# A one-core decode kernel of four layers: 30 K/V slots filled by halves, and an order planned with clocks of queues and fetches

## Chip, core and metric

One core of one Trainium2 chip. The metric is the device time of one execution in microseconds; three runs of the kernel before gave 314.23 (median), 312.15 and 315.84.

## What is computed

Eight independent rows `x` of 448 numbers (bf16) pass through attention, an MLP, the same attention and the same MLP. Weights and caches are shared by both rounds.

```python
W = min(4096, max(256, Sk // 4))                  # 1024 of 4096 positions
q = (x @ wq)                                      # 16 heads of 256
k, v = the last W rows of the caches              # 8 K/V heads, each for two q heads
p = _softmax(q k^T * Dh ** -0.5); o = p v
A(x) = o @ wo;   B(x) = _silu(x @ w1) @ w2        # F = 1792
x = x + A(_layernorm(x)); x = x + B(_layernorm(x))
x = x + A(_layernorm(x)); x = x + B(_layernorm(x))
```

K and V of one row are 16 blocks of 1024 x 256 numbers, 0.5 MB each: 67 MB in all, beside 10.55 MB of weights. Both attention rounds of a row use the same blocks, so each is loaded once.

## The kernel before

**Staging.** The weights stay in SBUF. K and V blocks go through 27 slots (`R`, L271). The loads are issued by SP in a fixed sequence (`pump`, L818): wq, the 8 K blocks of row 0, wo, its 8 V blocks, w1 and w2, then K and V of row 1 and so on. Load n takes the slot of load n-27 and waits for that slot's last reader. `load_k` (L432) writes runs of 4 KB, `load_v` (L438 and L444) runs of 1 KB, each with one transfer a slot. A V slot holds 256 positions of four heads (heads 0 to 3) or one whole head (4 to 7).

**One row, or batch.** `layer1` (L831) transposes the K slots in place on VectorE (L839, 16 halves), makes scores (`scores`, L570; eight matmuls of 256 columns, four at a time in quarters of the array), softmax (L580: row maximum, two small 32x32 transposes, exp, four transposes of the probabilities, sums), then p v. Heads 0 to 3 go by rows (`pv_rows`, L627), heads 4 to 7 by columns (`pv_cols`, L656: V is the weight operand, 16 matmuls a head, then an eviction L662 and that head's share of wo, L699). `chain` (L719) goes on from wo's four partial rows: `fold` (L711) evicts them (L713) and adds them into columns of 112 numbers, mean and variance come from small matmuls (L670, L678), 1/sqrt from Ln and Exp on ScalarE (L684, L686), w1 from 56 matmuls of 32 columns (`proj`, L468), silu from exp, a copy and a reciprocal (L733 to L738), w2 by rows (L741), `fold` again, then q of the second round: wq (L755) in two halves, each evicted (L760), turned (L763), copied (L766), spread (L549) and masked (L553). Layer-2 scores free the K slots, `pv_rows` of layer 2 the V slots. After row 7 the last wo, MLP and the output are made for all 8 rows together (`final_wo` L770, `final_rows` L779).

**Order.** Every operation is a task with an engine, a duration, reads and writes. `Plan.schedule` (L78) ranks the tasks by the longest path behind them, with fixed latencies between engines, and places each in the earliest gap of its engine; `emit` (L167) writes every engine's list with semaphore waits. Each engine runs its list in order. While PE would be idle in the chain, `keep` (L704) puts in matmuls that add zero.

Of the kernel before, what the change touches and what calls it, by code (L numbers as in the profile page):

```python
# [6 lines left out]
BF16 = mybir.dt.bfloat16  # L7
F32 = mybir.dt.float32
U32 = mybir.dt.uint32
ALU = mybir.AluOpType  # L10
# [3 lines left out]
SEM_LAT = {"pe": 0.05, "dve": 0.04, "act": 0.04, "pool": 0.06, "sp": 0.06}  # L14
LAT = {"pe": 0.15, "dve": 0.07, "act": 0.09, "pool": 0.05, "sp": 0.0}
LOAD_MARGIN = 1.5


class Task:
    __slots__ = ("eng", "fns", "dur", "prio", "name", "deps", "idx", "ready", "end", "sem", "val",  # L20
                 "vc", "n_bytes", "start", "users", "rank")
# [9 lines left out]
class Plan:  # L31
# [3 lines left out]
    def __init__(self, nc):  # L35
        self.nc = nc
        self.tasks = []
        self.last_w = {}
        self.readers = {}
        self.dma_sems = {}  # L40

    def add(self, eng, fns, reads=(), writes=(), dur=0.1, prio=0.0, name="", n_bytes=0, dma_key=None):
# [5 lines left out]
        t.idx = len(self.tasks)  # L48
        t.sem = dma_key
# [13 lines left out]
        for k in writes:  # L63
            if k in self.last_w:
                dep(self.last_w[k], True)
            for r in self.readers.get(k, ()):
                dep(r, False)
# [10 lines left out]
    def schedule(self, dma_lat=2.1):  # L78


        tasks = self.tasks
# [5 lines left out]
        sp_next = [t for t in tasks if t.eng == "sp"]  # L87
        nxt = {}
        for a, b in zip(sp_next, sp_next[1:]):
            nxt[a.idx] = b  # L90
        for t in reversed(sorted(tasks, key=lambda t: t.idx)):
# [4 lines left out]
            if t.eng == "sp":  # L96
                own = t.dur
                t.rank = max(own + dma_lat + r, (own + nxt[t.idx].rank) if t.idx in nxt else 0.0)
            else:
                t.rank = t.dur + r  # L100
        gaps = {e: [[0.0, 1e9]] for e in ("pe", "dve", "act", "pool")}
        sp_pos, sp_free, dma_free = 0, 0.0, 0.0
        heap, seq = [], 0

        def push(t):
            heapq.heappush(heap, ((-t.rank if t.eng != "sp" else -1e9), t.idx, t))

        def ready_of(t):
            r = 0.0
            for o, raw in t.deps.values():  # L110
                if o.eng != t.eng or o.eng == "sp":
                    lat = LOAD_MARGIN if o.eng == "sp" and t.eng == "dve" else LAT[o.eng]
                    r = max(r, o.end + lat + SEM_LAT[t.eng])
                elif raw and t.eng in ("dve", "act"):
# [4 lines left out]

        for t in tasks:  # L120
            if n_left[t.idx] == 0 and t.eng != "sp":
                push(t)
        if n_left[sp_next[0].idx] == 0:
            push(sp_next[0])
        done = 0
        while heap:
            _, _, t = heapq.heappop(heap)
            r = ready_of(t)
            if t.eng == "sp":
                t.start = max(r, sp_free)  # L130
                sp_free = t.start + 0.6
                s = max(t.start + 0.3, dma_free)
                dma_free = s + t.dur
                t.end = dma_free + dma_lat
                sp_pos += 1
                if sp_pos < len(sp_next) and n_left[sp_next[sp_pos].idx] == 0:
                    push(sp_next[sp_pos])
            else:
                g = gaps[t.eng]
                for k, (g0, g1) in enumerate(g):  # L140
                    s = max(g0, r)
                    if s + t.dur <= g1 + 1e-9:
                        break
                t.start, t.end = s, s + t.dur
                new = []
                if s - g0 > 0.02:
                    new.append([g0, s])
                if g1 - t.end > 0.02:
                    new.append([t.end, g1])
                g[k:k + 1] = new  # L150
            done += 1
            for u in succ[t.idx]:
                n_left[u.idx] -= 1
                if n_left[u.idx] == 0:
                    if u.eng != "sp":
                        push(u)
# [748 lines left out]
```

## Time and profile before

| | |
|---|---|
| median of three runs | 314.23 us |
| profiled execution, first to last instruction (span) | 307.8 us |
| profiled execution, its own time | not listed apart from the span |
| PE / VectorE / ScalarE / GpSimd busy | 218.9 / 147.1 / 69.3 / 10.5 us |
| moved by SP's queue | 77.68 MB, packets' time 73.3% of the span |
| granted PE clock, mean | 0.839 |

Engines are PE (matmul; PEld its weight loads), DVE (VectorE), ACT (ScalarE), POOL (GpSimd), SP. A row of a group reads: line, engine, operation, output<-inputs, shapes, count | busy us, mean ns of one | idle time of the engine just before and what ended it. A window row reads: from:to, length, busy time and count of the five engines (PE, PEld, DVE, ACT, POOL), granted clock, share of the 16 DMA engines, GB/s. A wait row reads: total us, times, longest. An arrow names what ended a wait.

### The profile page before, as it was taken

The numbers are of one execution on the slowest core, as the hardware profiler recorded it, in microseconds if no ns is written. First come the engines' busy times: TensorE is split into PE (matmuls) and PEld (weight loads), VectorE is DVE, ScalarE is ACT, GpSimd is POOL, SyncE is SP. The second block draws the span as 40 slices with busy tenths as digits, with TensorE's granted clock in tenths as the row PEclk, the third lists the DMA queues.
The fourth block names the chain that finished last, engine by engine and source line by source line (L and its number), as shares of the span: only waits on it lengthen the run. The fifth ranks groups of instructions, "written<-read, shape, count | busy, mean of one in ns | idle before, by whom it ended". The sixth has DMA issues, their size and how long they took to land.

```text
span 307.8 us, 9763 instructions
## 1 busy us (share of the span) xinstructions
PE 218.9 (71%) x4402; PEld 126.5 (41%) x4402; DVE 147.1 (48%) x436; ACT 69.3 (23%) x203; POOL 10.5 (3%) x22
## 2 busy tenths in 40 slices
PE   1052357675798778868796968788878897888683
PEld 1051113433454456345434634554455345443363
DVE  6049400158317934882487269427744674111113
ACT  2000100121312240423132223312231224022111
POOL 0002000000000000010001000000000000000000
PEclk9999999998675999799579999985799579657555
DMA  7999999999995199949955994999099919000000
GB/s 202 292 399 385 372 348 266 333 405 352 372 402 192 21 355 404 317 138 372 402 192 169 377 398 155 308 399 371 21 317 403 365 35 321 5 2 2 0 5 1
DMA packets 49977, 78.30 MB, mean 254 GB/s; under 512 B 2176, under 2 KB 40848, under 8 KB 49488
## 3 DMA queue, kind: packets, MB, share of 16 engines
q1 hardware_dynamic: 49936, 77.68, 73.3%
q8 instruction: 34, 0.56, 0.8%
q14 instruction: 7, 0.06, 0.0%
HBM read 77.67 MB, written 0.01 MB: 252 GB/s over the span
## 4 chain that ended last, share of the span: by engine, by line
PE 53%; DVE 14%; SPq 13%; ACT 10%; DMA 5%; issue 5%; ACTq 0%
PE bank L627 9%; SPq L444 8%; PE bank L468 7%; PE bank L570 6%; PE bank L699 5%; DVE slot L839 5%; PE bank L755 5%; DMA w_sb<-in_B_w_dram 5%; PE bank L656 4%; PE bank L706 4%; PE bank L741 4%; SPq L432 2%; ACT e_sb L590 2%; DVE qbd L553 2%; PE bank L595 2%
## 5 line engine op out<-in xcount | busy, mean ns | idle before, releaser
L839 DVE STREAM_TRANSPOSE slot<-slot 128x512 uint32<-128x512 uint32 x128 | 81.9, 686 | 9.4 <-DMA slot<-in_A_k_cache_dram 9.2
L570 PE MATMUL bank<-slot,qbd 128*8 128x256 bf16 x1024 | 41.0, 300 | 19.6 <-DVE mseg L576 8.9
L570 PEld LDWEIGHTS bank<-slot,qbd 128*8 128x8 bf16 x1024 | 24.7, 90 | 30.9 <-DVE mseg L576 10.1
L627 PE MATMUL bank<-slot,pT_sb 128*2 128x256 bf16 x768 | 30.6, 304 | 6.8 <-DMA slot<-in_A_v_cache_dram 3.9
L706 PE MATMUL bank<-sel,cols_b 128*128 128x480 bf16 x64 | 27.3, 524 | 2.6 <-DVE vneg L729 2.6
L590 ACT ACTIVATE e_sb<-bank,mb 128x256 bf16<-128x256 f32 x32 | 13.4, 471 | 42.9 <-DVE mb L586 42.8
L627 PEld LDWEIGHTS bank<-slot,pT_sb 128*2 128x2 bf16 x768 | 16.6, 88 | 14.8 <-DMA slot<-in_A_v_cache_dram 5.5
L713 ACT ACTIVATE rowb<-bank 128x448 bf16<-128x448 f32 x16 | 8.7, 544 | 61.9 <-PE bank L699 44.8
L699 PE MATMUL bank<-wo_sb,oT 128*1 128x448 bf16 x256 | 21.4, 435 | 1.6 <-issue 0.9
L656 PE MATMUL bank<-pT_sb,slot 128*128 128x2 bf16 x512 | 17.6, 164 | 4.2 <-issue 2.9
L656 PEld LDWEIGHTS bank<-pT_sb,slot 128*128 128x128 bf16 x512 | 15.3, 98 | 12.3 <-issue 9.9
L755 PE MATMUL bank<-wq_sb,xn 112*1 112x512 bf16 x256 | 20.3, 448 | 0.1
L608 DVE TENSOR_REDUCE l_sb<-bank 128x16 f32<-128x64 f32 x16 | 3.6, 225 | 35.0 <-PE bank L603 26.6
L468 PE MATMUL bank<-xbt,w_sb 112*128 112x32 bf16 (+1 forms) x504 | 16.7, 182 | 3.2 <-ACT xbt L722 1.9
L576 DVE TENSOR_REDUCE mseg<-bank 128x1 f32<-128x256 f32 x32 | 13.1, 413 | 11.3 <-PE bank L570 11.3
L662 DVE TENSOR_TENSOR oT<-bank,rl_sb 128x4 bf16<-128x4 f32 x32 | 5.2, 163 | 25.6 <-PE bank L656 25.6
L538 POOL TENSOR_TENSOR qbd<-q1s,mask 128x256 bf16<-128x256 bf16 x16 | 9.8, 613 | 215.4 <-PE bank L570 192.9
L640 DVE TENSOR_TENSOR oT<-bank,rl_sb 128x16 bf16<-128x16 f32 x24 | 5.0, 208 | 25.4 <-PE bank L636 24.8
L468 PEld LDWEIGHTS bank<-xbt,w_sb 112*128 112x128 bf16 x504 | 15.1, 102 | 4.0 <-ACT xbt L722 2.4
L760 ACT ACTIVATE rowb<-bank,rstd 128x512 bf16<-128x512 f32 x16 | 11.0, 687 | 20.1 <-PE bank L755 20.1
L634 ACT ACTIVATE o_sb<-bank 128x256 bf16<-128x256 f32 x24 | 9.2, 384 | 27.5 <-PE bank L627 27.2
L595 PE MATMUL bank<-ident,e_sb 128*128 128x128 bf16 x64 | 7.2, 243 | 11.1 <-ACT e_sb L590 11.1
(117 smaller groups left out, 195.5 us busy)
## 6 DMA issues: line engine op xcount, KB each, us to landing
slot<-in_A_k_cache_dram SPq DMA_DIRECT2D x64, 512.0 KB, 11.0
slot<-in_A_v_cache_dram SPq DMA_DIRECT2D x64, 512.0 KB, 8.6
wq_sb<-in_A_wq_dram SPq DMA_DIRECT2D x4, 896.0 KB, 9.7
wo_sb<-in_A_wo_dram SPq DMA_DIRECT2D x1, 3584.0 KB, 26.9
w_sb<-in_B_w_dram SPq DMA_DIRECT2D x2, 1568.0 KB, 16.4
qbd<-in_A_x_dram SPq DMA_DIRECT2D x1, 7.0 KB
out_dram<-e_sb SPq DMA_DIRECT2D x1, 7.0 KB
```

The costliest lines, as they stand in the source:

```text
L444: dma(lambda e: e.dma_start(slots[s][:, :].rearrange("v (j n) -> v j n", j=4), src.rearrange("j (v uh) d -> v j (uh d)", uh=2)), [("slot", ...
L468: fns.append(lambda e, o=o, i=i: e.matmul(bank[bank_i][:, col + (o - outs[0]) * n:col + (o - outs[0] + 1) * n], lhs(o, i), rhs(i).broadcas ...
L570: fns.append(lambda e, cb=cb, par=par, j=j, kvh=kvh, kv=kv: e.matmul(bank[sc][32 * j:32 * j + 8, k2 * 256:(k2 + 1) * 256], qbd[qi][:, kvh, ...
L576: dve(lambda e: e.tensor_reduce(mseg[layer][:, k2:k2 + 1], bank[sc][:, k2 * 256:(k2 + 1) * 256], AX.X, ALU.max, negate=True), bk(sc), [("m ...
L590: act(lambda e, k2=k2: e.activation(e_sb[ei][:, k2, :, :].rearrange("p uh (jj ul) -> p uh jj ul", ul=4), bank[sc][:, k2 * 256:(k2 + 1) * 2 ...
L595: pe([lambda e, c=c: e.matmul(bank[lb][:].bitcast(BF16)[:, c * P:(c + 1) * P], e_sb[ei][:, c // 2, c % 2, :], ident[:, :], is_transpose=Tr ...
L627: fns.append(lambda e, q=q, uh=uh, j=j, vv=vv: e.matmul(bank[ob][32 * j:32 * j + 2, c0:c0 + DH], pT_sb[ei][:, k2 * 2 + uh, j * 8 + 2 * q:j ...
L656: fns.append(lambda e, a=a, q=q, uh=uh: e.matmul(bank[vb][:, c0 + 2 * a:c0 + 2 * a + 2], vs[:, (2 * q + uh) * DH + a * P:(2 * q + uh) * DH ...
L699: fns.append(lambda e, i=i, c=c, kvh=kvh: e.matmul(bank[XB][32 * c:32 * c + 1, 0:D], oT1[:, i % 2, i // 2:i // 2 + 1], wo_sb[:, i * D:(i + ...
L706: pe([lambda e: e.matmul(bank[YB][:, 32:512], zero_b.broadcast_to([P, P]), sel[:].rearrange("p c m -> p (c m)")[:, 0:480], start=False, st ...
L755: pe([lambda e, j=j, c=c, k2=k2, wb=wb: e.matmul(bank[wb][32 * j:32 * j + 1, :], xn[0:CP, c:c + 1], wq_sb[0:CP, c, (4 * k2 + j) * 512:(4 * ...
L839: dve(lambda e, v=v: e.transpose(v, v), [("slot", s)], [("slot", s)], 0.67, prio, "KT")
```

## The change

- **Slots and loads.** 30 slots in one ring tensor. Each slot is filled by two transfers of 256 KB, with runs of 2 KB for both K and V. A half's load also waits until the half ten places ahead of it has landed (`ahead`), so at most ten are under way. V blocks are all whole heads. wo is loaded after the first V. wq and w1 lie on 128 partitions (448 = 3 x 128 + 64, the last part folded in two), wo in pairs of rows, w2 in one run a partition.
- **Norms.** Column sums of the weights carry the mean (q and w1 are made from x as it is, and mean times column sum is added behind). The variance comes from one set of matmuls; 1/sqrt from an integer guess and two Newton steps, on VectorE for the MLP, on GpSimd for attention, where it is applied as the scale of exp and not to q.
- **MLP.** w1 by rows: x is the weight operand, 16 matmuls of 448 columns, four at a time, and one 32x32 block transpose brings the result into columns. silu is tanh and one product.
- **Attention.** Scores of the first round: both halves in matmuls of 512 columns. p v by rows in matmuls of 512 columns (two positions at a time, added later); only head 7 of the first round goes by columns. q of the second round is turned by a block transpose of the PSUM bank. In row 7 the second round's softmax goes in two halves.
- **Shared homes.** Scratch tiles lie in K/V slots that are not in use at the start or the end, or in each other's place.
- **Order.** The planner follows a clock of 3.413 us windows for PE, a clock for each of 16 queues, and a cost for every 128 PE instructions fetched. It runs forward once, ranks the tasks by a backward run (`tails`) with written offsets by name and batch, runs again, and then applies a written list of moves. `fill` matmuls, which add zero, go where the plan has PE idle and the streamed columns of the last 3.4 us below a target; `keep` is left in the last row only.

```diff
+SEM_LAT = {"pe": 0.05, "dve": 0.05, "act": 0.05, "pool": 0.08, "sp": 0.1}
+LAT = {"pe": 0.17, "dve": 0.07, "act": 0.09, "pool": 0.08, "sp": 0.0}
+SWITCH = 0.1
+FETCH = (128, 1.4, 0.26)
+WINDOW, WARM, ACTIVE, PACED = 3.413, 43.0, 3072.0, 50.0
+FIRST, LANDED = 1.2, 1.5
+HOLDS = (("PVc0", 1, "oTc0", 1), ("s12", 1, "hT", 1), ("wq", 2, "qbd", 1))
+HELD = ("KT", "max0")
...
+    def tails(self, stay=0.3):
...
+    def best_schedule(self, filler):
+
+        self.schedule(filler, look=LOOKS[0])
+        tails = self.tails()
+        self.schedule(filler, {t.idx: tails[t.idx] + OFFSETS[max(0, t.batch - 5)].get(t.name.split(".")[0], 0.0)
+                               for t in self.tasks if t.idx in tails}, look=LOOKS[1])
+        for e, moves in MOVES.items():
+            by_idx = {t.idx: t for t in self.order[e]}
+            for pair in moves.split():
+                i, before = (int(x) for x in pair.split(":"))
+                self.order[e].remove(by_idx[i])
+                self.order[e].insert(self.order[e].index(by_idx[before]) if before >= 0 else len(by_idx), by_idx[i])
...
+                    queue = [max(t.start + FIRST, x) + t.dur for x in queue]
+                    t.end = max(queue) + LANDED
+                    release(t)
...
+                while n_fetch >= FETCH[0]:
+                    n_fetch -= FETCH[0]
+                    queue[n_block % 16] = max(queue[n_block % 16], best.start + FETCH[2]) + FETCH[1]
+                    n_block += 1
...
+    R = 30
+    PAD = 24
+    AHEAD, WHOLE = 10, 0
+    NJ, PAIR0, PAIR1, NR2, WQS = 3, 1, 0, 14, 0
...
+        if ahead:
+            n = n_bytes // (W * DH)
+            if len(started) > ahead - n:
+                t.deps[started[n - 1 - ahead].idx] = (started[n - 1 - ahead], True)
+            started.extend([t] * (n - 1))
...
     def load_k(s, b, kvh):
-        dma(lambda e: e.dma_start(slots[s][:, :].rearrange("p (u d) -> p u d", d=DH),
-                                  A_k_cache[b, kvh, S0:SK, :].rearrange("(p u) d -> p u d", p=P)),
-            [("slot", s)], W * DH * 2, "slot%d" % s)
-
+        for h in range(2):
+            dma(lambda e, h=h: e.dma_start(slots[s][:, 1024 * h:1024 * h + 1024], src[:, 1024 * h:1024 * h + 1024]),
+                [("slot", s, h)], W * DH, "slot%d_%d" % (s, h), rate=400e3, ahead=AHEAD)
...
+    def load_v(s, b, kvh):
+        src = A_v_cache[b, kvh, S0:SK, :].rearrange("(h p u) d -> h p (u d)", h=2, p=P)
+        for h in range(2):
+            dma(lambda e, h=h: e.dma_start(slots[s][:, 1024 * h:1024 * h + 1024], src[h]),
+                [("slot", s, h)], W * DH, "slot%d_%d" % (s, h), rate=400e3, ahead=AHEAD)
...
+    def rsqrt(eng, nv, y, t, nk, key, hold):
+
+        eng(lambda e: e.tensor_scalar(y.bitcast(I32), nv.bitcast(I32), -0.5, GUESS, op0=ALU.mult, op1=ALU.add),
...
+        one = len(nv.shape) == 2 and nv.shape[1] == 1
+        for i, c in enumerate(NEWTON):
+            if one and eng is dve:
+                eng(lambda e: e.scalar_tensor_tensor(out=t, in0=y, scalar=y, in1=nv, op0=ALU.mult, op1=ALU.mult),
+                    [(key, "y"), nk] + hold, [(key, "t")], 0.22, "nt")
...
+                eng(lambda e, c=c: e.scalar_tensor_tensor(out=y, in0=t, scalar=c, in1=y, op0=ALU.add, op1=ALU.mult),
+                    [(key, "t"), (key, "y")] + hold, [(key, "y")] + ([key] if i else []), 0.16, "ns")
...
+    def w1_rows(bi, lhs, n, key_of, name):
+
+        for i, c0, c1 in ((0, 0, 4), (1, 0, 4), (2, 0, 4), (3, 0, 2), (3, 2, 4)):
+            k = part(i, c0 > 0)
+            pe([lambda e, i=i, k=k, c=c: e.matmul(
+                bank[bi][32 * c:32 * c + n, 0:FN], lhs(k),
+                w1_sb[:, i * F + c * FN:i * F + (c + 1) * FN] if i < 3 else
+                w1_sb[:, 3 * F + c % 2 * FN:3 * F + (c % 2 + 1) * FN],
+                start=(i == 0), stop=(i == KC - 1), tile_position=(0, 32 * c)) for c in range(c0, c1)],
+               key_of(k) + W1_R, bk(bi), (FN, 4), name)
...
+    def turn(bi, dst, reads, writes, name):
+
+        dve(lambda e: e.transpose(dst.rearrange("p h (j i) -> p h j i", i=32),
+                                  bank[bi][:, 0:FN].rearrange("p (i h j) -> p h j i", h=2, i=32)),
+            bk(bi) + reads, writes, 0.18 + FN / 950.0, name)
...
+                        kv = ring[:, s:e_:st, :].rearrange("p s (u cb jj par) -> p cb par s u jj", u=8, cb=4, par=2)
+                        kv, m = kv[:, cb, par], 8 if ks[-1] == 0 else 16
+                        fns.append(lambda e, cb=cb, par=par, j=j, kv=kv, m=m, c0=c0, c1=c1: e.matmul(
+                            bank[sc][32 * j:32 * j + m, c0:c1],
+                            qbd[layer][:, j * 8 + cb * 2 + par].rearrange("p k x -> p (k x)")[:, 0:m], kv,
+                            start=(cb == 0 and par == 0 and c0 == lo), stop=(cb == 3 and par == 1),
+                            tile_position=(0, 32 * j), skip_group_check=True))
...
+            for u in (0, 2):
+                fns = []
+                for uh in range(u, u + 2, w):
+                    for j in range(nj):
+                        vv = slots[slot_of[b, "v", 4 * k2 + j]][:, (qh * 4 + uh) * DH:(qh * 4 + uh + w) * DH]
+                        fns.append(lambda e, qh=qh, uh=uh, j=j, vv=vv: e.matmul(
+                            bank[ob][32 * j:32 * j + 2 * w, 0:w * DH], p_col(ei, k2, j, qh, uh, w), vv,
+                            start=(qh == 0 and uh == 0), stop=(qh == 1 and uh == 4 - w), tile_position=(0, 32 * j)))
+                pe(fns, [("slot", slot_of[b, "v", 4 * k2 + j], qh) for j in range(nj)] + [("pT", ei, k2)], bk(ob),
...
+        pe([lambda e, c=c: e.matmul(s12, xbt[:, c, 0:1].broadcast_to([P, P]),
+                                    xbt[:, c, :].unsqueeze(2).broadcast_to([P, 2, XW]),
+                                    start=(si == 1 and c == 0), stop=False, skip_group_check=True)
...
+        act(lambda e: e.activation(th[:], vt[:], ACTF.Tanh, scale=rstds[0][:, 0:1]), ["vt", ("rstd", 0)], ["th"], 0.31, "tanh")
+        dve(lambda e: e.tensor_scalar(zh[:], vt[:], rstds[0][:, 0:1], None, op0=ALU.mult), ["vt", ("rstd", 0)],
+            ["zh"], 0.234, "zh")
+        dve(lambda e: e.scalar_tensor_tensor(out=hT[:], in0=th[:], scalar=1.0, in1=zh[:], op0=ALU.add, op1=ALU.mult),
+            ["th", "zh"], ["hT"], 0.17, "hT")
...
+                        fns.append(lambda e, j=j, c=c, wb=wb, off=off, h0=h0, n=n, k2=k2: e.matmul(
+                            bank[wb][32 * j:32 * j + 4, h0:h0 + n], xn[:, part(c, k2), j, :],
+                            wq_sb[:, off:off + n], start=(c == 0), stop=(c == KC - 1),
+                            tile_position=(0, 32 * j), skip_group_check=True))
+                dve(lambda e, wb=wb, h0=h0, n=n: e.transpose(
+                    qT[:, h0:h0 + n].rearrange("p (c a i) -> p c a i", a=2, i=32),
+                    bank[wb][:, h0:h0 + n].rearrange("p (c i a) -> p c a i", a=2, i=32)),
+                    bk(wb), (QT0 if h0 == 0 else []) + (QT1 if h0 + n > DH else []), 0.18 + n / 950.0, "qT")
...
+        nj = 3 if b == NB - 1 else NJ
...
+    fills = {n: [lambda e, j=j, m=P // n: e.matmul(
+        bank[OB[0]][m * j:m * j + m, 0:2 * DH], zero_b.broadcast_to([P, m]), wq_sb[:, 0:2 * DH], start=False, stop=True,
+        skip_group_check=True, **({"tile_position": (0, m * j)} if m < P else {})) for j in range(n)] for n in (1, 2, 4)}
+    fill = (fills, 0.214, 2 * DH,
+            lambda n: n.startswith("PV0.") and n.endswith(".0"), "oevh")
+    pl.best_schedule(fill)
+    first = pl.order["pe"][0]
+    first.fns = [lambda e: e.matmul(bank[YB][0:32, 0:1], ident[:, 0:32], ident[:, 0:1], start=True, stop=True)] * PAD + first.fns
+    pl.fill = fill
```

More of the change, by code (lines that the diff above doesn't have):

```diff
@@ L48, in add @@
         t.idx = len(self.tasks)
+        t.batch = self.batch
         t.sem = dma_key
@@ L163, in schedule @@
+        assert done == n_all, "no task can run"
+        order["sp"] = sp
+        self.order = order
         self.span = max(t.end for t in tasks)
-        self.busy = {e: sum(t.dur for t in self.order[e]) for e in self.order}
-        return self.order
+        self.busy = {e: sum(t.dur for t in order[e]) for e in order}
+        return order
     def emit(self):
@@ L562, in scores @@
+    QB1 = [("qbq", 0, q) for q in range(4)]
+    def scores(b, layer, ks, sc):
+        lo, hi = ks[0] * 256, ks[-1] * 256 + 256
         for cb in range(4):
             fns = []
[L564 to L573 removed]
```

1248 lines of the change are left out of this document (749 added, 499 removed), and 45 rows, old and new, of tables (MOVES, OFFSETS).

## Prediction

> **What bounds the kernel now.** I read the page first: its slices, then its queues.
>
> ```profile
> span 307.8 us, 9763 instructions
> ...
> PEclk9999999998675999799579999985799579657555
> DMA  7999999999995199949955994999099919000000
> GB/s 202 292 399 385 372 348 266 333 405 352 372 402 192 21 355 404 317 138 372 402 192 169 377 398 155 308 399 371 21 317 403 365 35 321 5 2 2 0 5 1
> ...
> q1 hardware_dynamic: 49936, 77.68, 73.3%
> ```
>
> A slice is 7.7 us. The transfers run without a break for twelve slices, then stop once in every batch, and the last six slices (46 us) have none. The median run, 314.23 us, lies 6.4 us above the span of 307.8; the runs shown, 312.15 to 315.84, put that at 4.4 to 8.0. The sum below is made on the span, and 6.4 is added.
>
> Why the transfers stop is in the waits of SP's own queue and in its timeline (start, length, line):
>
> ```profile
> SPq L444 <- PE bank L570: 57.5, 5, 15.1
> ```
>
> ```profile
> 105.71 0.37 SPq L444 DMA_DIRECT2D slot<-in_A_v_cache_dram  x1
> 106.12 3.00 SPq L438 DMA_DIRECT2D slot<-in_A_v_cache_dram  x4
> 109.17 6.07 SPq L432 DMA_DIRECT2D slot<-in_A_k_cache_dram  x8
> 115.28 18.98 SPq L444 DMA_DIRECT2D slot<-in_A_v_cache_dram  x4
> 134.30 2.71 SPq L438 DMA_DIRECT2D slot<-in_A_v_cache_dram  x4
> ...
> 252.22 2.40 SPq L438 DMA_DIRECT2D slot<-in_A_v_cache_dram  x4
> ```
>
> With 27 slots, load n takes the slot of load n-27. So the fourth V load of batch b+1 (L444) waits for K slot 0 of batch b, which is free when layer-2 scores (L570) are done. That V is needed for batch b+1's own chain, which ends in its layer-2 scores: a loop of one batch. From 106.12 to 252.22 it turns five times: 29.2 us each.
>
> **The loop in two parts.** First the loads. V loads issued at 106.1 to 108.5 land after (issue to landing, the four of L438 there):
>
> ```profile
> DMA to landing us min/median/max: 5.8/7.2/7.9
> ```
>
> so the last V is there at about 116, 10 us after the release at 105.7. Then the chain, from 116 to the next release at 134.3, 18 us:
>
> ```profile
> 118.01 0.26 PE L656 MATMUL bank<-pT_sb,slot 128*128 128x2 bf16 x5 [0.64 <-issue]
> ...
> 120.15 0.55 ACT L713 ACTIVATE rowb<-bank 128x448 bf16<-128x448 f32 x1 [4.86 <-PE bank L699]
> ...
> 123.18 0.23 DVE L729 SCALAR_TENSOR_TENSOR vneg<-ncs,nmean,bank 128x14 f32<-128x14 f32 x1
> ...
> 125.02 1.66 PE L741 MATMUL bank<-w_sb,hT 128*1 128x448 bf16 x14 [0.16 <-DVE hT L738]
> ...
> 126.71 0.54 ACT L713 ACTIVATE rowb<-bank 128x448 bf16<-128x448 f32 x1 [2.29 <-PE bank L741]
> ...
> 128.71 1.03 PE L755 MATMUL bank<-wq_sb,xn 112*1 112x512 bf16 x16
> ...
> 131.85 0.65 PE L570 MATMUL bank<-slot,qbd 128*8 128x256 bf16 x16 [0.52 <-DVE qbd L553]
> ```
>
> **Part 1 of the change: the loads.** Rates by kind of transfer, from windows in which one kind runs (last three columns: clock, DMA share, GB/s): wq; K; wo; V; w1 with w2.
>
> ```profile
> 2.50:15.00 12.50, 0.84 (x16) 0.67 (x15) 4.49 (x30) 0.83 (x3) 0.00 (x0) 1.00 0.99 290
> 16.00:24.00 8.00, 4.78 (x161) 4.53 (x161) 4.47 (x8) 0.50 (x1) 0.15 (x1) 1.00 1.02 408
> 26.00:35.00 9.00, 3.76 (x64) 1.85 (x64) 6.98 (x14) 0.00 (x0) 1.17 (x2) 1.00 1.09 381
> 37.00:46.00 9.00, 4.09 (x62) 1.41 (x64) 0.81 (x4) 0.66 (x2) 0.00 (x0) 1.00 1.09 349
> 48.00:56.00 8.00, 4.46 (x58) 2.23 (x58) 0.87 (x5) 1.27 (x4) 0.00 (x0) 1.00 1.06 246
> ```
>
> K arrives in runs of 4 KB, a slot of 524,288 bytes in 1.285 us; V in runs of 1 KB, 1.502 us. All halves now have 2 KB runs. The 384 extra runs of V cost 0.217 us, so 128 extra cost 0.072: 1.357 us a slot (386 GB/s). Ends: all at K's rate, 164.5 us for 128 slots, all at V's, 192.3; I take 173.7. Weights (10.55 MB): at the old rates 12.7 + 9.6 + 13.0 = 35.3 us, at K's 25.9. wq and w1 now lie mostly on 128 partitions, wo has 1,792-byte runs, w2 runs of 12.5 KB, so most of it should go at about 386 to 408: I take 27.7. First byte at 2.5. Loads without a stall end at 2.5 + 27.7 + 173.7 = 204, landed at 205. The same sum for before is 2.5 + 35.3 + 64 x 2.787 = 216; they really end at 261 (the 260:262 row below moves half of a full 2 us), so 45 us are stalls.
>
> Issue is no bound as long as SP needs under 0.68 us a half, of which there are 256:
>
> ```profile
> L438 SPq DMA_DIRECT2D slot<-in_A_v_cache_dram x4: 507/508/627, 106.1 to 108.5; - x4
> ```
>
> 0.51 plus a second wait (the half ten places back) is about 0.6; at 0.75 a half the stream would need 192 instead of 174. Behind that wait stand only the later halves and, at the very end, the output.
>
> The Trainium skill ("DMA: Bandwidth & Descriptors", Bandwidth) speaks against halves: it fits a lone transfer as 2.0 us plus bytes over 436 GB/s and advises 1 MiB or more, by which 256 KB alone would run at about 100 GB/s and 256 in a row would need some 670 us. The K row above, 408 GB/s with 512 KB transfers queued, shows that the fixed part overlaps when several are under way, and I go by it.
>
> **Part 2: the loop.** With 30 slots the first load that needs a release is V 6 instead of V 3: two slots after it instead of five. A lone V slot issued at 251.8 landed after
>
> ```profile
> DMA to landing us min/median/max: 4.0/4.0/4.0
> ```
>
> which is 2.5 us beyond its 1.5 of moving, so release to last V is 2.5 + 2 x 1.36 = 5.2 us instead of 10. The chain, by the rows above:
> - 116 to 120.15: three late heads by columns, 16 matmuls and an eviction each with wo behind them, become one head (kvh 7) whose wo goes straight into the columns: 4.1 becomes about 1.9.
> - 120.15 to 123.18: 56 narrow w1 matmuls become 16 of 448 columns, four at a time (16 x 448 / 4 = 1,792 columns, 0.75 us), plus a transpose that the trace doesn't have. Nearest is L839 below, 0.686 for 512 columns, so 0.60, between 0.2 and 0.9. No change, 3.0.
> - 123.18 to 125.02: exp, copy, reciprocal, product become tanh and product: 1.8 becomes 1.1. Newton's five DVE steps (each like L681, 0.22, so 1.1 us) replace Ln and Exp on ACT beside w1's 0.75 and the transpose; if that cover is missing, 0.5 is late.
> - w2: 1.7 us at half clock, 0.95 at full; fold and xn 2.0, unchanged.
> - wq to scores, 3.1: eviction, turn and copy become one 512-column transpose and an addition, 3.3. Scores to release 2.4 becomes 1.9, since less of the next batch stands between.
>
> The sum is 1.9 + 3.0 + 1.1 + 0.95 + 2.0 + 3.3 + 1.9 = 14.2. The loop needs 5.2 + 14.2 = 19.4 us; 16 slots need 21.7. The transfers become the bound, with 2.3 us to spare.
>
> **Part 3: the engines at 21.7 us.**
>
> ```profile
> 106.10:134.30 28.20, 22.61 (x494) 13.28 (x494) 16.91 (x50) 8.09 (x24) 1.23 (x2) 0.94 0.86 300
> 260.00:262.00 2.00, 1.63 (x55) 1.27 (x47) 0.69 (x4) 0.77 (x2) 0.00 (x0) 1.00 0.54 166
> 262.00:286.10 24.10, 20.75 (x298) 9.58 (x296) 3.74 (x16) 4.78 (x15) 0.00 (x0) 0.60 0.01 3
> 286.10:307.80 21.70, 13.07 (x330) 9.62 (x330) 5.27 (x20) 3.41 (x11) 0.00 (x0) 0.50 0.01 2
> ```
>
> ```profile
> L839 DVE STREAM_TRANSPOSE slot<-slot 128x512 uint32<-128x512 uint32 x128 | 81.9, 686 | 9.4 <-DMA slot<-in_A_k_cache_dram 9.2
> ...
> L706 PE MATMUL bank<-sel,cols_b 128*128 128x480 bf16 x64 | 27.3, 524 | 2.6 <-DVE vneg L729 2.6
> ...
> L656 PE MATMUL bank<-pT_sb,slot 128*128 128x2 bf16 x512 | 17.6, 164 | 4.2 <-issue 2.9 <-DMA slot<-in_A_v_cache_dram 1.0 <-DVE oT L662 0.3
> ...
> L468 PE MATMUL bank<-xbt,w_sb 112*128 112x32 bf16 (+1 forms) x504 | 16.7, 182 | 3.2 <-ACT xbt L722 1.9 <-issue 1.0 <-ACT xbt L781 0.3
> ...
> L538 POOL TENSOR_TENSOR qbd<-q1s,mask 128x256 bf16<-128x256 bf16 x16 | 9.8, 613 | 215.4 <-PE bank L570 192.9 <-DVE q1s L526 22.4
> ...
> L681 DVE SCALAR_TENSOR_TENSOR vn<-bank,nmean,deps_sb 128x1 f32<-128x1 f32 x16 | 3.5, 218 | 2.5 <-PE bank L678 1.8
> ```
>
> PE is busy 22.6 us a batch. The keep matmuls (27.3 / 8 = 3.4) go, three quarters of L656 (17.6 / 8, so 1.6) and 1.1 of w1 (L468: nine rounds with w1's sums, 1.86 each, become 0.75): 16.5 are left, and fills go only where the plan leaves PE idle. DVE has 16.9; three transposes (0.60 + 2 x 0.69), Newton and variance (6 x 0.22) and three more operands' steps (0.7) add 4.0, eleven small ones like L681 go (2.4): 18.5 of 21.7. That is close, and a chain step that falls behind a K transpose waits up to 0.69. The second norm's nine POOL steps lie between a ninth of L538 and L538 each, 0.6 to 5.5 us; I take 1.8, hidden by wq and the transposes, since only the softmax scale and the second half's qbd behind them wait. For such bubbles, and a first loop that has to settle, I allow 3 us of stalls in all: the last V lands at 208.
>
> **Part 4: the tail.** Before, 261 to 307.8 is 46.8 us, at clocks 0.60 and 0.50. V to the end of layer-2 scores takes 25; in the steady loop the same takes 18 + 2, so 5 is clock. After: 14.2 + 1.9 = 16. From the scores on, 21.7 now:
>
> ```profile
> 294.67 0.60 PE L627 MATMUL bank<-slot,pT_sb 128*2 128x256 bf16 x8
> ...
> 303.16 1.57 PEld L468 LDWEIGHTS bank<-qbd,w_sb 128*128 128x128 bf16 x56 [2.54 <-DVE qbd L799]
> ```
>
> PV runs until 295.3, 9 us after the scores; with the two halves' softmax apart, only the second is left, about 5. wo by rows saves 1.1, the last w1 and silu 1.5, w2 0.8: 21.7 becomes 14.5. Sum 30.5; half clock, as before, costs up to 5 more. I take 32.
>
> The Trainium skill ("TensorE: Matmul & The Clock Gate", HAM oscillation) asks only for no PE gap above about 3.4 us. The trace disagrees: in the tail the 2.54 us in the last row is PE's longest, and the clock is at half. By that rule the tail would have nothing to win from a full clock, 5 us less gain.
>
> **Sum.** 208 + 32 = 240 of span, + 6.4 = 246.4: I forecast **246 us**, own range 236 to 258 (K's rate for all loads -9, old weight rates +8, a cold tail +5; V's rate for all loads, +19, lies in the wide range).
>
> **Rivals.**
> - *The loop stays the bound, at 25 us.* For: a static order makes every engine wait behind its neighbours' work, and DVE is at 85%. Against: 2.3 us to spare. Seven loops x 3.3 = 23: 269 us.
> - *The plan doesn't do what it says.* Its clocks miss the chip's, and the loop stays at 29.2: 7 x 7.5 = 52, 298 us.
> - *Slower: the cap of ten.* Ten halves under way, 256 halves, so the stream takes 25.6 times the time from issue to landing. The K loads issued from 109.2 had
>
> ```profile
> DMA to landing us min/median/max: 9.2/10.9/13.0
> ```
>
>   and 25.6 x 10.9 = 279 makes 2.5 + 27.7 + 279 + 32 + 6.4 = 348 us. It decides from 9.6 us a half. Against: those had four megabytes queued ahead of them, ten halves are 2.6 MB, 6.8 us, and a lone load took 4.0. This is the mechanism by which the skill's size rule would matter.
> - *Better:* K's rate, short weights and no stall: 2.5 + 25.9 + 164.5 + 31 + 6.4 = 230.
>
> **How the numbers follow.** Forecast 0.60, loop at 25 us 0.22, plan fails 0.07, slower 0.05, better 0.06. 236 to 276 holds the first two. 1% (3 us) is about what a measurement of this kernel can tell from no change. All cases but the slower one end well below that: faster 0.93, same 0.02, slower 0.05.
>
> **What would show it.** Right: DMA near 9 in every slice up to 205 to 210 us, no long SP wait for layer-2 scores, K and V windows at about 386 GB/s, DVE at 18 to 19 us of a 22 us batch, keep rows nearly gone, the last 32 us without transfers at a clock above 0.8. Wrong: slices with 1 to 5 in the DMA line after slice 12; SP waits for its own transfers with the DMA share below 0.9 (the cap); gaps in DVE before the qT transposes (the loop).

## The result, and the profile after

The changed kernel takes **242.01 us** (median of 4 runs, 241.37 to 243.05) against 313.19 (310.79 to 315.84, 4 runs): ratio 0.7738, 95% interval 0.7694 to 0.7783. The forecast was 246, own range 236 to 258. The profiled execution took 241.48 us with a span of 239.7. In this and every later ratio, executions more than 1.5% above the fastest of their kernel are left out, while medians and ranges keep all of them.

The page of the changed kernel, a slice being 6.0 us:

```profile
PEclk9999985999999999999999999999999999999999
DMA  6999999999999999999999999999999999200000
GB/s 228 373 355 403 404 402 384 378 374 406 402 405 403 403 402 404 398 350 379 360 400 402 371 373 379 376 368 377 358 399 399 397 330 399 102 3 3 4 3 1
...
ring<-in_A_k_cache_dram SPq DMA_DIRECT2D x128, 256.0 KB, 6.2
```

The same bytes (77.69 MB) now pass without a stop: DMA stands at 9 from slice 2 to 34, the clock is near full, and the end with next to no transfers is 33 us instead of 46. A K half lands 6.2 us after its issue. The waits of SP's queue:

```profile
SPq L713 <- PE bank L951: 12.6, 6, 3.1
SPq L719 <- PE bank L881: 8.6, 5, 1.9
```

The wait for layer-2 scores was 57.5 us, the longest 15.1; now (L881) it is 8.6 and 1.9. SP's timeline (start, length; sixteen halves a row):

```profile
68.58 11.25 SPq L713 DMA_DIRECT2D ring<-in_A_k_cache_dram  x16
79.88 10.26 SPq L719 DMA_DIRECT2D ring<-in_A_v_cache_dram  x16
...
179.41 12.09 SPq L713 DMA_DIRECT2D ring<-in_A_k_cache_dram  x16
191.55 10.81 SPq L719 DMA_DIRECT2D ring<-in_A_v_cache_dram  x16
```

A row takes (179.41 - 68.58) / 5 = 22.2 us; it was 29.2. From VectorE's timeline, by the first-round maximum (L892), which I use as the mark of a row below:

```profile
91.63 0.69 DVE L892 TENSOR_REDUCE mrow<-bank 128x2 f32<-128x512 f32 x1 [0.83 <-POOL qbd L1129]
...
113.52 0.69 DVE L892 TENSOR_REDUCE mrow<-bank 128x2 f32<-128x512 f32 x1 [1.15 <-PE bank L881]
...
180.90 0.69 DVE L892 TENSOR_REDUCE mrow<-bank 128x2 f32<-128x512 f32 x1 [1.17 <-PE bank L881]
```

four rows in 89.27 us, **22.32 us a row**. Windows of the changed kernel: one row, then the tail in two parts (busy PE, PEld, DVE, ACT, POOL; clock, DMA share, GB/s).

```profile
114.00:136.00 22.00, 20.27 (x385) 9.48 (x379) 16.69 (x46) 9.80 (x34) 2.61 (x11) 1.00 1.04 388
...
205.00:222.00 17.00, 16.28 (x339) 8.95 (x339) 5.92 (x24) 7.98 (x29) 2.22 (x12) 1.00 0.03 10
222.00:240.00 18.00, 13.35 (x282) 7.66 (x281) 7.08 (x30) 5.24 (x18) 0.38 (x1) 1.00 0.01 3
```

The last V halves are issued from 200.6 to 201.9 us and land after

```profile
DMA to landing us min/median/max: 4.3/4.6/4.8
```

so the transfers end at some 206.5. In the row PE is busy 20.3 of 22 us. The fill matmuls alone (L1290) in the same row are 3.3 of it:

```profile
114.00:136.00 22.00, 3.34 (x10) 1.00 1.04 388
```

All this looks as forecast: an unbroken stream, rows near 21.7 us. Whether the stream *sets* the row is another question, and most of the experiments go to it.

### The profile page after: what moved, and what is told of

The parts are those of the page before. It is cut to its first block, busy times and chain, and to the rows that moved or that the text cites. A ratio compares the mean times of both kernels' runs of the same rounds, so it can differ in the third digit from the quotient of the medians.

```text
span 239.7 us, 8472 instructions
## 1 busy us (share of the span) xinstructions
PE 194.1 (81%) x3567; PEld 97.3 (41%) x3567; DVE 152.8 (64%) x425; ACT 86.5 (36%) x292; POOL 26.0 (11%) x125
## 3 DMA queue, kind: packets, MB, share of 16 engines
q1 hardware_dynamic: 40304, 77.69, 87.2%
## 4 chain that ended last, share of the span: by engine, by line
PE 47%; DMA 19%; DVE 16%; ACT 7%; SPq 7%; issue 4%; POOL 0%; DVEq 0%; ACTq 0%
DMA ring<-in_A_k_cache_dram 10%; PE bank L951 9%; PE bank L881 7%; DMA w2o<-in_B_w_dram 6%; DVE ring L1246 6%; PE bank L1002 6%; PE bank L1290 5%; PE bank L1104 5%; PE bank L1115 3%; DMA ring<-in_A_v_cache_dram 3%; SPq L682 3%; ACT qT L912 2%; DVE mrow L892 2%; PE bank L918 2%; PE bank L958 1%
## 5 line engine op out<-in xcount | busy, mean ns | idle before, releaser
L1246 DVE STREAM_TRANSPOSE ring<-ring 128x512 uint32<-128x512 uint32 x128 | 81.4, 684 | 10.7 <-DMA ring<-in_A_k_cache_dram 10.7
L1290 PE MATMUL bank<-wq_sb,smalls 128*128 128x512 bf16 x129 | 38.6, 386 | 0.0
L881 PE MATMUL bank<-ring,qbd 128*16 128x512 bf16 (+2 forms) x768 | 35.8, 324 | 3.4 <-DVE ring L1246 2.3
L951 PE MATMUL bank<-ring,pT_sb 128*4 128x512 bf16 (+1 forms) x512 | 36.2, 378 | 0.1
L881 PEld LDWEIGHTS bank<-ring,qbd 128*16 128x16 bf16 (+1 forms) x768 | 19.6, 91 | 17.1 <-DVE qbd L1129 3.9
L858 ACT ACTIVATE qbd<-q1s 32x128 bf16<-32x128 bf16 x32 | 10.2, 320 | 42.9 <-PE bank L881 42.3
L892 DVE TENSOR_REDUCE mrow<-bank 128x2 f32<-128x512 f32 (+1 forms) x17 | 11.0, 646 | 11.9 <-PE bank L881 11.1
L1104 PE MATMUL bank<-wq_sb,xn 128*4 128x512 bf16 (+1 forms) x272 | 17.7, 369 | 0.9 <-ACT x2s L1091 0.5
L951 PEld LDWEIGHTS bank<-ring,pT_sb 128*4 128x4 bf16 (+1 forms) x512 | 11.5, 84 | 11.1 <-issue 1.8
L1290 PEld LDWEIGHTS bank<-wq_sb,smalls 128*128 128x128 bf16 x129 | 10.2, 98 | 12.3 <-issue 7.6
L1002 PE MATMUL bank<-w2o,oT 128*1 128x448 bf16 x224 | 13.2, 352 | 0.7 <-DMA w2o<-in_A_wo_dram 0.7
L1109 DVE STREAM_TRANSPOSE qT<-bank 128x512 f32<-128x512 f32 (+1 forms) x17 | 11.3, 664 | 2.2 <-PE bank L1104 2.0
L912 ACT ACTIVATE qT<-bank,mrow 128x256 bf16<-128x256 f32 x17 | 7.2, 470 | 7.6 <-DVE mrow L905 7.3
## 6 DMA issues: line engine op xcount, KB each, us to landing
w2o<-in_B_w_dram SPq DMA_DIRECT2D x1, 1568.0 KB, 14.5
```

Source lines behind the costliest of these rows:

```text
L881: fns.append(lambda e, cb=cb, par=par, j=j, kv=kv, m=m, c0=c0, c1=c1: e.matmul(bank[sc][32 * j:32 * j + m, c0:c1], qbd[layer][:, j * 8 + c ...
L892: dve(lambda e: e.tensor_reduce(mseg[layer][:, ks[0]:ks[-1] + 1], bank[sc][:, lo:hi].rearrange("p (k n) -> p k n", k=len(ks)), AX.X, ALU.m ...
L912: act(lambda e, k2=k2: e.activation(e_sb[ei][:, k2, :, :].rearrange("p uh (jj ul) -> p uh jj ul", ul=2), bank[sc][:, k2 * 256:(k2 + 1) * 2 ...
L951: fns.append(lambda e, qh=qh, uh=uh, j=j, vv=vv: e.matmul(bank[ob][32 * j:32 * j + 2 * w, 0:w * DH], p_col(ei, k2, j, qh, uh, w), vv, star ...
L1002: pe([lambda e, i=i, c=c: e.matmul(bank[XB][32 * c:32 * c + 1, 0:D], rhs(i), w_sb[:, i * D:(i + 1) * D], start=(first and i - i0 < 4), sto ...
L1104: fns.append(lambda e, j=j, c=c, wb=wb, off=off, h0=h0, n=n, k2=k2: e.matmul(bank[wb][32 * j:32 * j + 4, h0:h0 + n], xn[:, part(c, k2), j, :],
```

## The experiments

"Order kept" means that every engine's list is that of the changed kernel. Beside them the kernel before took medians of 312.4 to 315.9 us.

### How many slots: 27 with the order kept, 27 planned anew

```diff
+halves = [loads of slots, in order]
+for i, t in enumerate(halves[54:], 54):   # wait for the release that three slots fewer would need
+    t.deps.update({k: d for k, d in halves[i + 6].deps.items() if d[0].eng == "pe"})
```

> The kernel after with its order of every engine kept, but each load also waits for the release that it would need with 27 slots. Theory (27 slots made a loop of release, load and chain the bound; with 30 the transfers are): five slots instead of two lie behind the release, 5.2 + 4.1 + 14.2 = 23.5 us a row instead of 21.7, so 7 x 1.8 = 12 us more, 250 to 258 us. Rival A (slots do not matter, the shorter chain made the whole gain): 244 or less. Rival B (the loop is still the bound after): 7 x 4.1 = 28 more, 270.

Measured: **295.97 us** (292.33 to 298.52), above every expectation. The transfers are 35% of its chain, where the changed kernel has 19%. This order was made for 30 slots, and a load that comes late holds up, as I read it, not only its own row but all that stands behind it on PE and DVE. So the planner was run again, without its list of moves:

```diff
-MOVES = {"pe": "1800:-1 ...", ...}
+MOVES = {"pe": "", "dve": "", "act": "", "pool": "",}
...
-    R = 30
+    R = 27                                 # the second kernel only
```

> The changed kernel without the list of moved tasks: the order is the planner's own. Theory: the moves are polish of about 1 to 4% in an order whose period the transfers set: 243 to 250 us. Rival: the planner's own order leaves the loop bound on the release (25 us a row or more): 262 us or more.

> The changed kernel without the list of moves and with 27 slots instead of 30, planned anew for 27. Beside the 30 slots without moves it tells what three slots are worth in an order that knows of them. Theory: slack of 2.4 us of the loop against three slots of 1.3 us (about 4 us): the loop binds by 1.5 to 2 us a row, 10 to 14 us over the kernel with 30 slots and no moves, 253 to 264. Rival: the 296 us of the frozen order with 27 slots were the price of the slots themselves and not of an order that did not know of them: 285 or more. If it is within 3 us of the 30 slots, the slots aren't what the loop hangs on.

Measured: 30 slots without moves **248.80** (248.40 to 249.62; ratio 0.7990, 0.7949 to 0.8031), 27 slots **267.82** (266.22 to 269.69; ratio 0.8599, 0.8501 to 0.8697). SP's timeline of the second, then its chain by engine:

```profile
84.37 12.71 SPq L696 DMA_DIRECT2D ring<-in_A_v_cache_dram  x16
...
213.13 14.01 SPq L696 DMA_DIRECT2D ring<-in_A_v_cache_dram  x16
```

```profile
PE 38%; DMA 23%; DVE 20%; SPq 7%; issue 5%; ACT 5%; POOL 1%; DVEq 0%
```

and the timeline of the first:

```profile
81.68 10.38 SPq L696 DMA_DIRECT2D ring<-in_A_v_cache_dram  x16
...
198.22 10.47 SPq L696 DMA_DIRECT2D ring<-in_A_v_cache_dram  x16
```

25.75 us a row against 23.31; by the first-round maximum, over five rows, 26.0 against 23.0. So three slots are worth 19 us, 2.4 to 3 a row, where I had expected 10 to 14, and with 27 the transfers have a larger part in the chain (23% instead of 14%, SP's queue 7% instead of 5%). Three slots hold 3 x 1.30 = 3.9 us of stream (1.30 is 524,288 bytes at 404 GB/s). Since 2.4 to 3 came back, I estimate that the loop through the slots has 0.9 to 1.5 us to spare at 30 in the planner's own order; the two orders differ too, so this isn't shown. The moves are worth 6.8 us.

### A longer chain: copies ahead of the row eviction

```diff
 for t in pl.tasks:
     if t.name == "rowb":     # L1018, twice a row
+        t.fns = [8-column copy in the same bank] * n + t.fns      # n = 3, n = 8
```

> The kernel after with three small extra ScalarE copies ahead of each row eviction, about 0.6 us, so 1.2 us longer a row on the chain. Theory (transfers bind, 2.3 us to spare in the loop): only the last row shows it, 243 to 245 us. Rival B (the loop binds): 8 x 1.2, 250 to 252.

> The same with eight copies, about 1.6 us per eviction, 3.2 us a row. Theory: 3.2 in the last row and 7 x (3.2 - 2.3) = 6 before it, 248 to 254 us. Rival B: 8 x 3.2 = 26, 267.

Measured: **243.65** (243.48 to 244.78; ratio 0.7751, 0.7712 to 0.7789) and **250.57** (249.59 to 251.17; ratio 0.7960, 0.7919 to 0.8001). The totals fall where the theory of 2.3 us to spare put them, but for another reason, because the copies cost less than I had priced them. ScalarE's timeline with eight:

```profile
124.78 0.65 ACT L1301 ACTIVATE bank<-bank 128x8 f32<-128x8 f32 x8 [1.64 <-PE bank L1002]
125.25 0.63 ACT L1018 ACTIVATE qT<-bank 128x448 bf16<-128x448 f32 x1
```

They overlap: the eviction starts 0.47 us later and takes 0.63 instead of 0.54, 0.56 us more, 1.1 a row with two evictions. The row mark, from VectorE's timeline,

```profile
93.54 0.69 DVE L892 TENSOR_REDUCE mrow<-bank 128x2 f32<-128x512 f32 x1 [0.83 <-POOL qbd L1129]
...
187.08 0.69 DVE L892 TENSOR_REDUCE mrow<-bank 128x2 f32<-128x512 f32 x1 [1.16 <-PE bank L881]
```

gives 23.39 us a row over four rows, 1.07 more. **What is put into the chain comes out almost in full; there is nothing to spare.** With three copies, the same reading gives 0.4 us a row added and 0.29 out.

### 1 KB runs, and no cap

```diff
-src = A_v_cache[...].rearrange("(h p u) d -> h p (u d)", h=2, p=P)
+src = A_v_cache[...].rearrange("(h a p u) d -> h p a (u d)", h=2, a=2, p=P)   # V in runs of 1 KB
```

> The kernel after with V read in runs of 1 KB instead of 2 KB (other positions of the window meet p, so the output is another; bytes, transfers and order are the same). Theory (transfers bind): a V slot takes 1.50 us as before the change instead of 1.30, 64 x 0.20 = 13 us more, 252 to 256 us. Rival B or an engine as the bound: under 247.

Measured: **242.73** (242.31 to 244.43; ratio 0.7724, 0.7679 to 0.7769). The rival. A half lands some 6 us behind its issue, so a stretch that holds V alone begins some 5 us behind the first V issue. Such a window of this kernel:

```profile
63.00:73.00 10.00, 9.22 (x135) 4.43 (x137) 7.14 (x18) 2.90 (x9) 0.61 (x1) 1.00 1.09 382
```

and of the changed kernel, with 2 KB runs:

```profile
63.00:73.00 10.00, 9.22 (x141) 4.60 (x140) 6.76 (x17) 3.47 (x10) 0.61 (x1) 1.00 1.06 404
```

382 against 404 GB/s: runs of 1 KB cost some 5.5%, not the 15% between K and V of the kernel before. A V slot takes 1.37 us, not 1.50; the stream of a row becomes 8 x 1.30 + 8 x 1.37 = 21.4 us, still below the row's 22.3, and the time doesn't move.

```diff
 for t in pl.order["sp"]:
+    if t.name.startswith("slot"):      # no wait for the half ten places back
+        t.deps = {i: d for i, d in t.deps.items() if d[0].eng != "sp" or d[0].name == t.name}
```

> The changed kernel, same order, without the wait of each load for the load ten halves earlier: a load waits only for its slot. Theory: the cap costs nothing and gives nothing that shows, since the order in which halves are issued stays and the rate with ten under way is already that of the queue: 240 to 246 us. Rival (the slower one of the prediction): a half takes so long that ten under way hold back the rate: without the cap 236 or less. Second rival: more under way makes the halves land later and out of order, so that releases and chain are late: 247 or more.

Measured: **241.70** (241.01 to 242.43; ratio 0.7759, 0.7719 to 0.7799), no change. K halves land after 6.3 us instead of 6.2, and SP waits for slots instead of transfers:

```profile
SPq L713 <- PE bank L951: 15.2, 6, 3.0
SPq L719 <- PE bank L881: 10.2, 6, 3.0
```

With the cap these were 12.6 and 8.6. The releases of the slots pace the loads, so no queue builds up that a cap could cut. The chain of this run has 4% DMA, all of it at the start: with all its bytes the steady rows go by without a transfer in their chain.

### Fewer bytes

```diff
 for h in range(2):
-    dma(... slots[s][:, 1024 * h:1024 * h + 1024], src[h] ...)
+    n = 1024 if b < 2 else 768
+    dma(... slots[s][:, 1024 * h:1024 * h + n], src[h][:, 0:n] ...)    # K likewise
```

> From the third batch row on, each half of a K or V slot brings only the first three quarters of its columns; the last quarter keeps what an older row left there, so the output is another one. Order, instructions and waits are those of the changed kernel. Theory: the transfers set the row's period (22.2 us) and the loop from the release of a slot to the last V and through the chain needs about 2.4 us less (the slack that the lengthened chain showed), so the period of six rows falls by about 2.4 us and the time to 228 to 232 us; the stretches with little transfer grow. Rival: an engine, or the loop itself, binds at 22 us as it is: 238 us or more. Second rival: there is no such loop at work and the transfers are all that binds (a quarter of 22 us less a row): below 218 us.

Measured: **240.76** (240.55 to 242.02; ratio 0.7738, 0.7682 to 0.7794), by the ratio the time of the changed kernel. My theory falls, and the first rival's 238 or more holds. The page, first the rate, then the chain by engine:

```profile
GB/s 220 386 363 403 405 402 384 394 374 406 403 405 394 276 318 296 253 267 303 269 288 294 276 286 269 339 251 306 312 291 234 279 282 298 40 3 3 4 3 1
...
PE 59%; DVE 22%; ACT 9%; DMA 4%; issue 4%; SPq 2%; POOL 0%; DVEq 0%; ACTq 0%
```

From slice 14 to 34 the stream carries 234 to 339 GB/s, and next to nothing is gained. The row mark, from VectorE's timeline,

```profile
91.46 0.69 DVE L894 TENSOR_REDUCE mrow<-bank 128x2 f32<-128x512 f32 x1 [0.83 <-POOL qbd L1131]
...
180.27 0.69 DVE L894 TENSOR_REDUCE mrow<-bank 128x2 f32<-128x512 f32 x1 [1.16 <-PE bank L883]
```

gives 22.20 us a row, 0.12 less. The chain has 4% DMA, all of it at the start. In the steady rows it runs from one row's first-round maximum over softmax, p v, wo, the norm, the MLP, wq and the second-round scores (L881) to the first-round scores of the next row, which stand behind them in PE's list, and to their maximum. Transposes of K that stand ahead in VectorE's list are on it in some rows (L1248, 3.4 us from 98.45 on), and fills of PE's list as well (8.5% of the span). **One row's whole way through the engines is the row's time.** The transfers of full halves, 16 x 1.30 = 20.8 us, lie just under it. In one row they still bind: the changed kernel's chain has a K transfer of 6.4 us from 157.93 on, that row (157.83 to 180.90) takes 23.07 us, and with short halves 22.68, which is 0.39 of the 0.46 us that short halves gain over the four rows.

### Without the fills

```diff
+pe = pl.order["pe"]
+lo, hi = first task "S1.0", last task "PVc0.7"
+pl.order["pe"] = [t for t in pe if not (t.name == "fill" and lo <= its place < hi)]   # 81 of 129
```

> The changed kernel, same order, without the 81 fill matmuls between the first layer-2 scores and the last piece of layer-1 outputs (the other 48 stay). With quarter-short loads the time fell by 1.2 us only, so the transfers alone don't set the row, and in the windows TensorE is busy 20.1 of 22 us, 3.3 of it fills. Theory P: the order of TensorE with its fills is what sets the row beside the transfers, both at about 22 us; without fills the transfers are left: 238 to 242 us at an unchanged clock. Rival C: SP, which needs 0.62 us a half (19.8 us for 32) and waits for releases besides, sets the row and TensorE doesn't: 241 to 244. Rival H: the clock falls without fills and TensorE is at the bound: 248 or more.

> Both at once: halves of three quarters from the third row on (the output is another one) and no fill matmuls between the first layer-2 scores and the last piece of layer-1 outputs. Theory P: with the transfers and the fills both taken back, the row falls to what is left of TensorE's order or to SP's issue (some 20 us): 226 to 234 us. Rival C: SP's issue and its waits set the row already: 238 or more at an unchanged clock. Rival H: the clock falls: 245 or more.

Measured: **250.87** (249.23 to 255.23; ratio 0.7946, 0.7889 to 0.8003) and, with short halves as well, **252.36** (248.47 to 252.88; ratio 0.7952, 0.7853 to 0.8052): rival H. The clock line of the first, and a window of 4 us in it:

```profile
PEclk9999999999689768899995999597999899899999
```

```profile
134.00:138.00 4.00, 3.10 (x38) 1.07 (x34) 3.25 (x7) 1.14 (x7) 1.65 (x8) 0.50 1.05 405
```

The same stretch of time in the changed kernel, with fills:

```profile
134.00:138.00 4.00, 3.26 (x77) 1.96 (x69) 2.24 (x7) 2.02 (x6) 0.61 (x1) 1.00 1.04 348
```

The fills hold the clock and are worth 9 us by the medians, 6.5 by the ratios; with three quarters of the bytes the time without them is the same, so here too the transfers are not what binds. What PE's order, in whose chain the fills themselves stand, would need without them at full clock could not be had this way.

The cold window doesn't tell what made the clock fall. It fell at some 133 us; here are the 3 us in which it fell, and 3 us of the same run that no fall followed:

```profile
131.00:134.00 3.00, 2.05 (x32) 0.82 (x26) 3.00 (x7) 1.14 (x6) 0.00 (x0) 0.86 1.06 406
...
119.00:122.00 3.00, 1.68 (x40) 1.06 (x43) 1.71 (x7) 2.51 (x7) 0.00 (x0) 1.00 1.05 404
```

The Trainium skill ("TensorE: Matmul & The Clock Gate", HAM oscillation) warns of PE gaps above some 3.4 us. Here the clock fell though the longest gap in PE's timeline from 110 us to the fall is 1.05 us.

### A shorter chain

```diff
-                ACTF.Exp, bias=mb[ei][:, k2:k2 + 1],
+                ACTF.Exp,
...
+drop the tasks "max", "mT", "mg", "mb", "mbs" (L892, L900, L902, L905, L909) from every list
```

> The changed kernel, same order, without the row maximum: the exponentials take the scores as they are, and the reduction, the two small transposes and the fold before them (1.36 us from the first to the end of the last, 0.70 + 0.22 + 0.18 + 0.22 and their gaps, twice a row) are left out, on these inputs, whose scores are small. Eight added copies cost 1.1 us a row and the row grew by 1.07, and quarter-short loads shortened it by 0.12 us only. Theory E: a chain of engine work in TensorE's order sets the row (22.3 us), from one row's maximum to the next one's, and the transfers at 404 GB/s need some 20.8 us. Then the row falls by 1.2 to 1.36 us over seven rows, 8.4 to 9.5 us, and 2 to 4 us go in the last row's own two maxima: 228 to 233 us. Rival T: transfers and chain bind together at 22 us; then only the last row's part is gained: 237 to 241 us.

> Both: no row maximum, and from the third row on halves of three quarters (the output is another one). Theory E: as without the maximum, and at most a little more, since the chain is left at some 20.9 us and the transfers are far below it: 226 to 231 us, and no more than 3 us below the kernel with full halves. Rival T: the full halves held the row in the kernel without maxima: 6 us or more below it. Rival S: SP's issue (0.62 us a half, 19.8 us a row) with its waits holds both: the two agree within 1 us at 236 or more.

Measured: **239.14** (238.69 to 239.42; ratio 0.7611, 0.7585 to 0.7638) and **237.69** (237.50 to 237.95; ratio 0.7568, 0.7533 to 0.7603). Theory E missed its 9 us, though the two lie no more than 3 us apart, as it had them; rival T has the 239, but not the 6 us between the two. Rival S had the two within 1 us, and they are 1.45 apart. SP isn't at its limit, for it still waits 27 us for releases (second kernel):

```profile
SPq L714 <- PE bank L953: 14.2, 7, 3.0
SPq L721 <- PE bank L883: 12.8, 5, 3.1
```

The timelines say what happened. VectorE of the changed kernel:

```profile
135.85 0.69 DVE L892 TENSOR_REDUCE mrow<-bank 128x2 f32<-128x512 f32 x1 [1.13 <-PE bank L881]
...
137.03 0.21 DVE L905 STREAM_TRANSPOSE mrow<-mg 128x32 f32<-128x32 f32 x1
```

ScalarE of the changed kernel at the same time, with the exponentials (L912) of an earlier and a later row:

```profile
93.06 0.84 ACT L912 ACTIVATE qT<-bank,mrow 128x256 bf16<-128x256 f32 x2 [0.20 <-DVE mrow L905]
...
135.85 1.36 ACT L858 ACTIVATE qbd<-q1s 32x128 bf16<-32x128 bf16 x4 [4.82 <-PE bank L881]
137.28 0.84 ACT L912 ACTIVATE qT<-bank,mrow 128x256 bf16<-128x256 f32 x2
...
182.32 0.84 ACT L912 ACTIVATE qT<-bank,mrow 128x256 bf16<-128x256 f32 x2
```

ScalarE of the kernel without maxima:

```profile
92.42 0.66 ACT L912 ACTIVATE qT<-bank 128x256 bf16<-128x256 f32 x2
...
134.88 1.36 ACT L858 ACTIVATE qbd<-q1s 32x128 bf16<-32x128 bf16 x4 [4.81 <-PE bank L881]
136.27 0.66 ACT L912 ACTIVATE qT<-bank 128x256 bf16<-128x256 f32 x2
...
180.43 0.66 ACT L912 ACTIVATE qT<-bank 128x256 bf16<-128x256 f32 x2
```

Four copies of the next row's q (L858) wait for the same scores and stand ahead of the exponentials in ScalarE's list. They take 1.36 us, as long as the maximum with its small transposes (1.39). Without these the exponentials start 1.39 us behind the copies' start instead of 1.43. What is gained there is 0.04 and the 0.18 by which the exponentials got shorter, 0.22 a row. Over the four rows from the first to the last exponentials shown, the row is 22.00 us instead of 22.32; where the other 0.1 comes from I didn't find. Short halves then take another 0.1 a row. So the row is still the chain's, by its second branch. That moving L858 behind the exponentials would free the rest was not tried, so this branch is read from the timelines and not shown by a run. Both kernels are faster than the changed one, but leave out the maximum, which holds only for small scores.

## Why the prediction was right, and where its steps failed

The number was right, and the account of the loads was nearly right by size; the reason given for the row was wrong, and several errors that cancel helped the number.

- **The row's bound (wrong).** The step "the transfers become the bound, with 2.3 us to spare" failed twice. The transfers need 20.8 us and not 21.7, and the engines' chain needs 22.3 and not 19.4. A quarter fewer bytes gave 0.12 us a row, and 1.1 us put into the chain cost 1.07. Rival "loop stays the bound" had the right reason, the static order, though at 22.3 instead of 25 us and without the transfers in it; 25.75 is what a row costs with 27 slots in the planner's own order. That 22.3 and 21.7 lie close is why the total held, and that is luck.
- **The chain's parts (nearly right).** PE and ScalarE of the changed kernel, one row:

```profile
118.74 0.55 PE L985 MATMUL bank<-pT_sb,ring 128*128 128x32 bf16 x16
...
121.60 0.54 ACT L1018 ACTIVATE qT<-bank 128x448 bf16<-128x448 f32 x1 [1.64 <-PE bank L1002]
...
126.23 0.92 PE L1002 MATMUL bank<-w2o,hT 128*1 128x448 bf16 x14
127.19 0.54 ACT L1018 ACTIVATE qT<-bank 128x448 bf16<-128x448 f32 x1 [0.46 <-PE bank L1002]
128.55 1.03 PE L1104 MATMUL bank<-wq_sb,xn 128*4 128x512 bf16 x16
...
132.16 1.06 PE L881 MATMUL bank<-ring,qbd 128*8 128x256 bf16 x32
```

  From the column head to the release it is 118.7 to 133.2, 14.5 us against 14.2. The parts fit less well: 2.9 to the first eviction (step: 1.9), 4.6 to w2 (4.1), 1.0 for w2 (0.95), 1.4 to wq (2.0), 3.6 to the scores (3.3), 1.1 to the release (1.9). That their sum agrees is partly luck. What I left out is how a row is joined to the next: the first-round scores of row b+1 come behind the second-round scores of row b in PE's list, and softmax and p v follow. From the maximum at 113.52 to L985 at 118.74 that is 5.2 us, from the release to the next maximum at 135.85 another 2.6: 5.2 + 14.5 + 2.6 = 22.3. My loop had the wait for V in the place of these.
- **Rate (too low) and its reason (wrong).** 403 to 404 GB/s and not 386. Runs of 1 KB go at 382 here, so run length explains at most 26 of the 59 GB/s by which the old V rate, 349, lay below K's 408. What made V slower beyond that in the kernel before stays open. With the stalls the stream averages 384 GB/s from 41.5 to 205.5 us, near 386 for another reason.
- **Stalls.** The last V landed at some 206.5, and the step had 208. Behind that stand rows 1.5 us longer than the 20.8 of the stream, some 10 us in seven rows, in the place of 3 us in all; the faster stream (128 x 1.30 = 166 us and not 174) made up for them.
- **Engines.** PE without fills 20.3 - 3.3 = 17.0 a row (step: 16.5), DVE 16.7 to 17.2 (18.5).
- **Tail.** 239.7 - 206.5 = 33.2 us at clock 1.00, where 32 was taken with some allowance for a cold clock. The last layer-2 scores, in PE's timeline,

```profile
222.70 1.11 PE L881 MATMUL bank<-ring,qbd 128*16 128x256 bf16 x32 [0.54 <-DVE qbd L1129]
```

  end at 223.8: 17.3 us behind V (step: 16), with 15.9 left (14.5; the step's own terms, 21.7 less 4, 1.1, 1.5 and 0.8, give 14.3).
- **What lies around the span (mis-sized).** 6.4 us was the distance of the old median from another execution's span. The profiled execution here has 241.48 - 239.7 = 1.8, and every execution of these runs has 1.7 to 1.9. This term alone is the 4 us between 246 and 242; the span, 240 by the sum, came out at 239.7.
- **The cap (right).** Halves land after 6.2 us, below the 9.6 from which the cap would have bound; taking the cap away changes nothing. The Trainium skill ("DMA: Bandwidth & Descriptors", Bandwidth) advises 1 MiB or more a transfer; here 256 KB halves, about ten under way, carry 404 GB/s.
- **What was not tested.** Of the 71 us, 6.8 hang on the moves and 19 on the slots, both by the planner's own order. How the rest divides among halves, norms, MLP, attention and order was not taken apart.

## What to carry to other kernels

A stream that is busy at 9 in every slice isn't thereby the bound: take a quarter of its bytes away, or put a known delay into the chain, and see which of the two moves the row. In kernels whose engines run written lists, look for what joins one row to the next *in the list* and not only in the data, and before taking an operation off that path look for what stands beside it for as long. A change in slots has to be planned anew to be priced: the same 27 slots cost 19 us with their own order and over 50 with another's.

## What the runs showed of the hardware

- Small ScalarE operations on a PSUM bank, one behind the other, overlap: eight of 0.16 to 0.23 us each delayed the next one by 0.47 us.
- The granted clock fell to 0.50 near the end of 3 us in which PE was busy for 2.05 (32 matmul records) and without a gap above 1.05 us; 3 us with 1.68 busy (40 records) were followed by no fall. The share of busy time alone doesn't tell a cold stretch.
- At about ten 256 KB transfers under way, runs of 2 KB carried 404 GB/s and runs of 1 KB 382.
